# Re-ordering the fill work of a recurrent forward loop: unit scores, softmax and value products moved between the waits of a step, query turns taken off TensorE

## The chip, the cores and the metric

The program runs on one core of one Trainium2 chip. The metric is the device time of one launch in microseconds. Names of engines: PE is TensorE's matmul queue (PEld its weight loads), DVE is VectorE, ACT is ScalarE, POOL is GpSimd, SP is SyncE, which here only issues transfers. Lines such as L766 are lines of the kernel before.

## The reference

The kernel computes a forward pass and all its gradients. What matters here is one part of the forward pass, a recurrence over 64 segments of 32 tokens with a memory of 8 rows of width 640:

```python
for s in range(n_seg):                                   # 64 segments
    h = concat([mem, xs])                                # 8 memory rows + 32 tokens, 640 wide
    q, k, v = h @ Wq, h @ Wk, h @ Wv                     # 32 heads of 128
    p = softmax(where(mask, q @ k.T * Dh ** -0.5, -1e9)) # 40 x 40 for each head
    o = (p @ v) @ Wo
    mem = o[:8]                                          # the next segment needs these 8 rows
    outs.append(o[8:])
```

Each step needs the 8 memory rows that the step before produced. The token rows of a segment depend on the memory through keys and values alone, so most of their work can be done later.

## The kernel before, in words

Before the loop, queries, keys and values of the first 672 tokens are computed in full and stored in memory (QVX, KX). The loop (the function recurrence) has a chain for each of the 64 steps t. The chain takes hx, 32 columns: 8 memory rows and, riding along, 24 token rows of a later segment. It runs:

- projections (helper packed_half, L320, 20 matmuls of 512 columns for each half of a weight): first half of the values (sv0), two halves of the keys, two of the queries, second half of the values (sv1). Each half is copied out of its accumulator bank (bA, bB, bC) to a stage tile, and the stages are stored to QVS and KS by SP (the helper dump, L634);
- value_rows (L643), which puts the 8 memory rows of the values into the tile vt;
- packed_sel (L328), which turns the memory rows of keys and queries;
- the memory's own attention: scores (L676), copy sTm, turn (L686), softmax on DVE and ACT (the tile Pm, L697), turn (L311), values (L705), copies to oTm;
- the output projection, called the fold (L339, 64 matmuls), the sum of its halves fsz (L355), a turn (L370) and the copy into the next hx (L722).

Between these stand named gaps (W0, W1, V0, W2, G1 to G6). The function FILL puts other work into them, by the name of the gap. That work is the attention of the token rows, three segments to a tile and four heads to a unit (tile, quad): a tile of 120 rows has 8 units, and step t works on units of the tile before, by the table 0, 1, 2, then 3, 4, 5, then 6, 7. A unit goes through: ld of q and v rows (L265, L777, L245), turn_q (four PE turns of the queries, L788, and an ACT copy), scores (L800 to L805), soft_max and soft_exp (L813, L835), norm (L855, on POOL) with a store to PR, turn_p (L868), pv_mm (L888, L891), pv_turned and pv_rows with stores to OTX and OR. Keys of a later tile come by ld_k (tile kr, L265) and are turned by kprep (L766). The tiles oride and ride bring token columns for oTm and hx. Single matmuls on the identity (L945, the table WARM) are also put into gaps; nothing reads their result.

in_order fixes the order in which the code was written on each engine's queue, so every engine, SP with its transfers too, handles its instructions strictly one after the other, and one that waits holds up all behind it. The transfers issued by SP and ACT share eight completion counters in turn. The tile tag "oride" is one buffer for three things in a step: the stage sv0, then the loaded oride, then half of the fold's sum.

Of the kernel before, what the change touches and what calls it, by code (L numbers as in the profile page):

```python
# [9 lines left out]
BF16 = mybir.dt.bfloat16  # L10
# [6 lines left out]
P = 128  # L17
# [297 lines left out]
def packed_half(k, bank, x, W, b):  # L315

    for dc in range(k.DC):
# [258 lines left out]
def recurrence(k, W0, W4, Wv, Wk_, Wq, Wo, own, ps, banks):  # L576
    nc, tc = k.nc, k.tc
    D, DC, S, H, HD, T = k.D, k.DC, k.S, k.H, k.HD, k.T
    with tc.tile_pool(name="achain", bufs=1) as ch, \
# [7 lines left out]
        WARM = dict(G2=1, G3=2, G5=2)  # L587
# [33 lines left out]
        def chain(t, gap):  # L621
# [14 lines left out]
            def values(b, sv, bank):  # L636
                packed_half(k, bank, hx, Wv, b)
                k.copy(sv, bank[:], eng='s')
# [12 lines left out]
            dump(sv0, k.QVS[t // 4, :, :, t % 4, 1, 0:512])  # L651
            sq = stage()
            half(Wq, 0, sq, bA)
            dump(sk[:], k.KS[t // 4, :, :, t % 4])
            half(Wq, 1, sq, bB)
            qmT = ch.tile([P, H, 8], BF16, name="qmT", tag="fup")
            for sg, b_, dst, eng in ((sk, bC, kT[:, :, 40 * s:40 * s + 8], 's'), (sq, bA, qmT[:], 'v')):
                pk = bview(b_, P, 8, 4, 8)
                packed_sel(k, pk, sg, 0)
                packed_sel(k, pk, sg, 1)  # L660
                k.copy(dst.rearrange("p (g j) c -> p j g c", g=4), pk[:], eng=eng)
                if sg is sk:
                    gap("W1")
            dump(sq[:], k.QVS[t // 4, :, :, t % 4, 0])
            gap("V0")
            sv1 = stage()[:, 0:512]
            values(1, sv1, bC)
            value_rows(1, sv1)
            gap("W2")

            psT = bview(bA, P, 2, 8, 16)
            for h in range(H):
# [3 lines left out]
                nc.tensor.matmul(psT[0:m, h // 16, :, h % 16], k.kTT[:, o:o + m], qmT[:, h, :], start=True, stop=True)  # L676
            sTm = ch.tile([P, 2, P], BF16, name="sTm", tag="fup")
            nc.scalar.copy(sTm[:], psT.rearrange("p a q h -> p a (q h)"))
            if t + 1 < T:
                ride(t + 1)  # L680
            gap("G1")
            if t > 0:
                qm(t - 1)
# [69 lines left out]
        uu = {}  # L753

# [6 lines left out]
        def kprep(tl, qd, eng='s'):  # L761
            ns, nm, nx, n = k.geo(tl)
            kr = uu.pop(("kr", tl, qd))
            pt = ps.tile([P, 4, nx], BF16, name="kpt", tag="x", bufs=5)
            for j in range(4):
# [1556 lines left out]
```

## Time and profile before

| what | value |
|---|---|
| median of 3 runs | 4611.26 us (4608.62 to 4618.95) |
| the profiled execution's own time | 4624.73 us, its span 4623.0 us |
| granted TensorE clock, whole span | 0.983 |
| steps 0 to 63 of the loop | about 440 to 1540 us of the span |
| in 440 to 1540 us: busy PE, DVE, ACT, POOL | 997.8, 737.9, 593.0, 629.8 us of 1100 |
| transfers there | 0.63 of the transfer engines' time, 180 GB/s |

A row of the timeline gives start, duration, engine, line and operation, with the idle time before it and what ended it in brackets; rows of one form may be merged (x20). A PE duration includes the tail of the pipeline, so what a group costs in the queue is the distance from its start to the next start. Rows named SPq are transfers being issued; the duration is that of issuing, not of landing. Some matmul records are missing from a trace.

### The profile page before, as it was taken

Reading aid. Unit: us, or ns where it says so; the run is one execution under the profiler, and the core shown is the slowest. Engines: PE = TensorE matmul, PEld = TensorE weight load, DVE = VectorE, ACT = ScalarE, POOL = GpSimd, SP = SyncE. Lnnn points to the kernel's source line nnn. Section 1 sums busy time; section 2 is a strip of 40 time slices with the busy share of each in tenths; the row PEclk is TensorE's granted clock in tenths of the full one; section 3 lists DMA queues with packets and bytes.
Section 4 is the critical chain, followed back from the end, with each engine's and each line's share of the span. In section 5 each row is a group of like instructions: output and inputs, shape, how many; then the busy total and the mean of one; then the engine's idle time right before and its main releaser. Section 6 shows DMA issues by size and latency. Waiting matters only on the chain. (4 is left out here: it accounts for less than half of the span.)

```text
span 4623.0 us, 155683 instructions
## 1 busy us (share of the span) xinstructions
PE 4302.4 (93%) x62114; PEld 2828.5 (61%) x62336; DVE 2251.9 (49%) x7137; ACT 1615.4 (35%) x4509; POOL 2110.7 (46%) x3531
## 2 busy tenths in 40 slices
PE   8998998899999887999999998999999999999999
PEld 4544665565665545666666666577656766667665
DVE  8734666666666534555555553244223432311550
ACT  5532555555554523333333332133222322200000
POOL 6532555555565413555555554355334543211440
PEclk9999999999999998999999999999999999999999
DMA  7773666666665668788777776555435644589774
GB/s 263 241 253 110 183 180 180 185 182 184 182 180 171 169 156 240 220 230 226 222 224 219 221 206 163 114 159 148 128 105 141 163 130 110 154 227 211 166 173 100
DMA packets 986047, 834.55 MB, mean 181 GB/s; under 512 B 519914, under 2 KB 875694, under 8 KB 983360
## 3 DMA queue, kind: packets, MB, share of 16 engines
q1 hardware_dynamic: 754855, 531.10, 42.2%
q0 software_dynamic: 129952, 228.13, 17.0%
q10 hardware_dynamic: 100515, 65.34, 5.3%
q8 instruction: 493, 8.08, 0.7%
q14 instruction: 232, 1.90, 0.1%
HBM read 472.66 MB, written 310.33 MB: 169 GB/s over the span
## 5 line engine op out<-in xcount | busy, mean ns | idle before, releaser
L1697 PE MATMUL wg<-gr,hr 128*128 128x512 bf16 x2352 | 519.1, 379 | 2.5
L1678 PE MATMUL g<-land,ghacc 128*128 128x320 bf16 x3072 | 459.0, 300 | 0.8
L320 PEld LDWEIGHTS <-hx 128*32 128x32 bf16 x10240 | 266.5, 97 | 264.7 <-issue 27.5
L1697 PEld LDWEIGHTS <-hr 128*128 128x128 bf16 x2400 | 233.9, 98 | 278.9
L1678 PEld LDWEIGHTS <-ghacc 128*128 128x128 bf16 x3072 | 288.9, 98 | 103.8 <-ACT ghacc L92 2.2
L90 DVE CAST wgo<-wg 128x512 bf16<-128x512 f32 x72 | 49.8, 692 | 471.2 <-PE wg L1697 471.2
L908 POOL DMA_DIRECT2D OR<-xv x163 | 94.5, 580 | 335.6 <-ACT xv L92 290.5
L92 ACT COPY ghacc<-t6g 128x768 bf16<-128x768 bf16 (+1 forms) x176 | 137.2, 780 | 295.2 <-PE t6g L1660 284.8
L339 PEld LDWEIGHTS <-gkv 128*8 128x8 bf16 x8192 | 189.8, 87 | 81.9 <-issue 2.3
L1643 POOL DMA_DIRECT2D GSP<-grs x48 | 25.6, 543 | 456.4 <-ACT grs L1635 454.6
L628 DVE CAST stg<-bank 128x512 bf16<-128x512 f32 x256 | 168.4, 688 | 124.8 <-PE bank L320 108.5
L1354 POOL DMA_DIRECT2D VTD<-gvT x176 | 130.2, 749 | 198.4 <-ACT gvT L1353 182.5
L1684 DVE TENSOR_TENSOR ghacc<-ghacc,g 128x320 f32<-128x320 f32 x192 | 93.7, 488 | 209.8 <-PE g L1678 209.8
L92 ACT CAST wgo<-wg 128x512 bf16<-128x512 f32 x48 | 28.1, 586 | 479.8 <-PE wg L1697 406.9
L835 ACT ACTIVATE xP<-xsp,xnm 120x120 bf16<-120x120 f32 (+1 forms) x540 | 186.0, 367 | 17.8 <-DVE xnm L817 15.1
L855 POOL TENSOR_TENSOR xP<-xP,xrz 120x480 bf16<-120x480 bf16 x163 | 163.8, 1020 | 49.2 <-DVE xrz L854 39.4
L339 PE MATMUL bank<-Wo,oTm 128*32 128x320 bf16 x4032 | 159.2, 313 | 15.3 <-DVE oTm L90 14.1
L320 PE MATMUL bank<-WoT,hx 128*32 128x512 bf16 x2560 | 154.1, 388 | 11.3 <-DVE hx L1312 10.9
L1401 POOL DMA_DIRECT2D GXP<-gks x157 | 93.1, 593 | 155.4 <-ACT gks L1399 154.7
L320 PE MATMUL bank<-Wv,hx 128*32 128x512 bf16 x2560 | 161.6, 381 | 1.1 <-DVE hx L722 1.1
L351 ACT COPY fup<-bank 64x160 f32<-64x160 f32 (+1 forms) x190 | 57.4, 334 | 293.2 <-PE bank L339 288.5
L245 POOL DMA_DIRECT2D land<-QVS x256 | 144.9, 570 | 30.4 <-DMA land<-GOS 5.8
(399 smaller groups left out, 10924.5 us busy)
## 6 DMA issues: line engine op xcount, KB each, us to landing
kTT<-VTD SPq DMA_DIRECT2D x64, 320.0 KB
PR<-xP POOLq DMA_DIRECT2D x168, 120.0 KB, 3.0
VTD<-gvT POOLq DMA_DIRECT2D x168, 120.0 KB, 4.2
land<-DSR SPq DMA_DIRECT2D x168, 120.0 KB
land<-PR SPq DMA_DIRECT2D x168, 120.0 KB
OR<-xv POOLq DMA_DIRECT2D x163, 120.0 KB, 3.7
orr<-OR SPq DMA_DIRECT2D x14, 1280.0 KB
KS<-stg SPq DMA_DIRECT2D x64, 256.0 KB
```

Source lines behind the costliest of these rows:

```text
L92: return nc.scalar.copy(out, in_)
L245: eng.dma_start(d, src if src.shape[0] > 1 else src[0])
L320: k.nc.tensor.matmul(bank[32 * g:32 * g + 32, :], x[:, dc, :], W[:, dc, c0:c0 + 512], start=(dc == 0), stop=(dc == k.DC - 1), tile_positio ...
L339: k.nc.tensor.matmul(pm[a][p0:p0 + nq, 0:320], x[:, h, :], W[:, h, 320 * b:320 * b + 320], start=(first and i == 0), stop=(last and i == 1 ...
L628: nc.vector.tensor_copy(sg[:, b * 512:(b + 1) * 512], bank[:])
L835: nc.scalar.activation(Pb[0:n, j, 0:n], sp[0:n, j, :], ACT.Exp, bias=nmx[0:n, j:j + 1], scale=k.scale, accum_out=Z[0:n, j:j + 1])
L855: eng.tensor_tensor(Pb[0:n, :, 0:n], Pb[0:n, :, 0:n], bc_last(rz[0:n], n), ALU.mult)
L908: q.dma_start(k.OR[120 * tl:120 * tl + n, c0:c0 + 512], v[0:n])
L1354: nc.gpsimd.dma_start(k.VTD[tl][:, :, h0:h0 + 4, :], vTq[:])
L1678: nc.tensor.matmul(pg[:], ring[:, i, j, r0:r0 + P], Ws[qd][i][:, j, 320 * h:320 * h + 320], start=(i == 0 and j == 0), stop=(i == 2 and j ...
L1684: nc.vector.tensor_tensor(a, a, pg[:], ALU.add)
L1697: nc.tensor.matmul(pw[:], hr[:, tl, dc * P:(dc + 1) * P], grs[i][:, tl, :], start=(tl == 0), stop=(tl == NF - 1))
```

## The change

It rewrites FILL and what FILL calls; the arithmetic of the chain stays.

- Scores of the units of step t+1 are issued in G5 and G6 of step t (the wait for the fold's sum) rather than in G2 of their own step. Their softmax runs while the projections run (S0 to W3), with one exponential for each head in every unit; the variant with a subtraction for the third unit goes. Turns of the probabilities, value products and their stores come into G1 to G4.
- The queries of a unit are no longer loaded as rows and turned on PE: SP issues a crossbar transfer (DMA_TRANSPOSE) from QVS or QVX for 96 columns, and POOL copies the 24 memory columns from a tile qTm that the chain now keeps (q_mem).
- The memory rows of sv0 reach vt by four SP transfers rather than four DVE copies, and they stand ahead of the store of sv0.
- kprep of two units moves from G4 to G2, into bank bB, ahead of the turn of Pm (L311). The identity matmuls of G5 and, in steps with units, of G2 go.

```diff
-        WARM = dict(G2=1, G3=2, G5=2)
+        WARM = dict(G2=1, G3=2)
+        qTm = [ch.tile([P, H, 24], BF16, name=f"qTm{i}") for i in range(2)]
...
             def value_rows(b, sv):
                 for g in range(4):
                     p0, c0 = 64 * (g // 2), (g % 2) * 1024 + b * 512
-                    (nc.gpsimd if b == 1 and g % 2 else nc.vector).tensor_copy(vt[p0:p0 + 8, c0:c0 + 512], sv[32 * g:32 * g + 8])
+                    dst, src = vt[p0:p0 + 8, c0:c0 + 512], sv[32 * g:32 * g + 8]
+                    if b == 0:
+                        nc.sync.dma_start(dst, src)
+                    else:
+                        (nc.gpsimd if g % 2 else nc.vector).tensor_copy(dst, src)
+            gap("S0")
             sv0 = ch.tile([P, 512], BF16, name="sv0", tag="oride")[:]
-            values(0, sv0, bA)
+            packed_half(k, bA, hx, Wv, 0)
+            k.copy(sv0, bA[:], eng='s')
+            value_rows(0, sv0)
+            dump(sv0, k.QVS[t // 4, :, :, t % 4, 1, 0:512])
+            gap("S1")
             sk = stage()
             half(Wk_, 0, sk, bB)
-            value_rows(0, sv0)
             half(Wk_, 1, sk, bC)
             gap("W0")
...
+        def kprep(units, bank=None, eng='v'):
...
+            pt = ps.tile([P, m, nx], BF16, name="kpt", tag="x", bufs=5)[:] if bank is None else bview(bank, P, m, nx, bf=True)
...
+        def ld_q(tl, qd):
...
+            turned_load(k, qTs[i][:, :, 0:nx], src)
+        def q_mem(tl, qd, eng='g'):
...
+            k.copy(qTs[i][:, :, nx:n], qTm[tl % 2][:, 4 * qd:4 * qd + 4, 0:nm], eng=eng)
...
+            if g == "S0":
+                for i in range(3):
+                    at(soft_max, t, i)
+                at(lambda a, b: soft_exp(a, b, 0, 2), t, 0)
+                if t > 0:
+                    qm(t - 1)
+                at(ld_q, t + 1, 0)
...
+            elif g == "W0":
+                at(lambda a, b: norm(a, b, q=None), t, 0)
+                for i in range(2):
+                    at(ld_v, t, i)
+                at(norm_st, t, 0)
+            elif g == "W1":
+                at(lambda a, b: norm(a, b, q=None), t, 1)
+                at(norm_st, t, 1)
                 oride_ld(t)
+                at(ld_q, t + 1, 1)
...
+            elif g == "W4":
+                at(norm_st, t, 2)
                 ride_ld(t + 1)
+                at(ld_v, t, 2)
                 for u in kb[0:2]:
                     ld_k(*u)
+                at(ld_q, t + 1, 2)
             elif g == "G1":
+                at(lambda a, b: turn_p(a, b, 's'), t, 0)
+                at(lambda a, b: turn_p(a, b, 's'), t, 1)
                 oride(t)
...
+                at(pv_mm, t, 0)
+                at(pv_mm, t, 1)
+                at(turn_p, t, 2)
+                if kb:
+                    kprep(kb[0:2], bB)
+                at(pv_turned, t, 0)
+                at(pv_rows, t, 0)
...
+                for u in kb[2:]:
+                    kprep([u])
+                at(scores, t + 1, 0)
+                at(scores, t + 1, 1)
             elif g == "G6":
-                at(turn_p, t, 1)
-                at(pv, t, 0)
-                at(norm, t, 2)
+                at(scores, t + 1, 2)
```

Three places show how the order of instructions moves. The first is SP's queue in the middle of the loop, from the store of sv0 to the key rows kr of the same step. Before:

```order
L634 DMA QVS<-sv_19845 128x512
L634 DMA KS<-stg 128x1024
L634 DMA QVS<-stg 128x1024
L874 DMA oride<-OTX 128x768
L265 DMA kr<-KS 96x512 x2
```

In the change, from the four transfers of value rows to kr:

```order
L642 DMA vt<-sv_19576 8x512 x4
L635 DMA QVS<-sv_19576 128x512
L801 DMA xv<-QVM 24x512
L265 DMA xv<-QVS 96x512
L801 DMA xv<-QVM 24x512
L265 DMA xv<-QVS 96x512
L875 DMA oride<-OTX 128x768
L270 DMA_TRANSPOSE xqT_2978<-QVS 128x4x96
L635 DMA KS<-stg 128x1024
L635 DMA QVS<-stg 128x1024
```

and right behind these, in the same step:

```order
L801 DMA xv<-QVM 24x512
L265 DMA xv<-QVS 96x512
L265 DMA kr<-KS 96x512 x3
L635 DMA QVS<-stg 128x512
```

Between the store of sv0 and the first kr stood three transfers; now there are ten (eight in the steps with two units), one of them a crossbar turn. The load of oride writes the buffer that sv0's store and the four value transfers read, so it waits until all five have landed.

The second place is PE around the turn of Pm (L311). Before, key turns (kpt) come behind the memory's values (L705):

```order
L705 LDWEIGHTS vt
L705 MATMUL bank_4108<-PTm,vt 128x16
L766 LDWEIGHTS kr
L766 MATMUL kpt<-ident,kr 128x96
...
L339 LDWEIGHTS oTm
L339 MATMUL bank_4107<-Wo,oTm 32x320
```

In the change they come ahead of L311:

```order
L869 LDWEIGHTS xP_2983
L869 MATMUL xpp<-ident,xP_2983 128x120
...
L777 LDWEIGHTS kr
L777 MATMUL bank_4108<-ident,kr 128x96
...
L311 LDWEIGHTS Pm
L311 MATMUL bank_4109<-ident,Pm 128x128
```

The memory's chain (L311, then L705) now stands in PE's queue behind instructions that wait for the transfers of kr.

The third place is PE behind the fold. Before, turns of queries (qpt) and of probabilities (xpp) stood there:

```order
L788 LDWEIGHTS xq
L788 MATMUL qpt<-ident,xq 128x120
...
L868 LDWEIGHTS xP_2981
L868 MATMUL xpp<-ident,xP_2981 128x120
...
L370 LDWEIGHTS fsz
L370 MATMUL bank_4109<-sel,fsz 128x8
```

In the change a third key turn and the next step's scores:

```order
L777 LDWEIGHTS kr
L777 MATMUL kpt<-ident,kr 128x96
L815 LDWEIGHTS ident
L815 MATMUL xsp<-mask_88,ident 128x480
L818 LDWEIGHTS xqT_2980
L818 MATMUL xsp<-kTT,xqT_2980 128x24
```

The turns of queries are gone from PE's queue here, and more matmuls than before stand between the fold and the turn of its sum (L370).

More of the change, by code (lines that the diff above doesn't have):

```diff
@@ L312, in turn_pad, with packed_half @@
     k.nc.scalar.copy(dst[:].rearrange("p a q h -> p a (q h)"), ps3)
-def packed_half(k, bank, x, W, b):
-    for dc in range(k.DC):
+def packed_half(k, bank, x, W, b, d0=0, d1=None):
+    for dc in range(d0, k.DC if d1 is None else d1):
         for g in range(4):
@@ L652, in chain @@
             sq = stage()
             half(Wq, 0, sq, bA)
+            gap("W1")
+            pk = bview(bC, P, 8, 4, 8)
+            packed_sel(k, pk, sk, 0)
+            packed_sel(k, pk, sk, 1)
+            k.copy(kT[:, :, 40 * s:40 * s + 8].rearrange("p (g j) c -> p j g c", g=4), pk, eng='s')
             dump(sk[:], k.KS[t // 4, :, :, t % 4])
             half(Wq, 1, sq, bB)
[L656 to L663, printed above, removed]
+            pq = bview(bA, P, 8, 4, 8)
@@ L664, in chain @@
+            packed_sel(k, pq, sq, 0)
+            gap("W2")
+            sv1 = stage()[:, 0:512]
+            packed_half(k, bC, hx, Wv, 1, 0, 2)
+            packed_sel(k, pq, sq, 1)
+            qm_ = qTm[tl % 2][:, :, 8 * s:8 * s + 8]
+            k.copy(qm_.rearrange("p (g j) c -> p j g c", g=4), pq, eng='v')
+            packed_half(k, bC, hx, Wv, 1, 2, k.DC)
+            k.copy(sv1, bC[:], eng='s')
             dump(sq[:], k.QVS[t // 4, :, :, t % 4, 0])
-            gap("V0")
-            sv1 = stage()[:, 0:512]
@@ L667, in chain @@
-            values(1, sv1, bC)
+            gap("W3")
             value_rows(1, sv1)
-            gap("W2")
+            gap("W4")
             psT = bview(bA, P, 2, 8, 16)
@@ L675, in chain @@
                 o += 120 * H * (tl % 2)
-                nc.tensor.matmul(psT[0:m, h // 16, :, h % 16], k.kTT[:, o:o + m], qmT[:, h, :], start=True, stop=True)
+                nc.tensor.matmul(psT[0:m, h // 16, :, h % 16], k.kTT[:, o:o + m], qm_[:, h, :], start=True, stop=True)
             sTm = ch.tile([P, 2, P], BF16, name="sTm", tag="fup")
             nc.scalar.copy(sTm[:], psT.rearrange("p a q h -> p a (q h)"))
+            gap("G1")
             if t + 1 < T:
                 ride(t + 1)
-            gap("G1")
-            if t > 0:
-                qm(t - 1)
             ps2 = bview(bA, P, 2, 40)
@@ L759, in ld_k @@
             uu["kr", tl, qd] = kr
-        def kprep(tl, qd, eng='s'):
+        def kprep(units, bank=None, eng='v'):
+            tl, qd = units[0]
             ns, nm, nx, n = k.geo(tl)
-            kr = uu.pop(("kr", tl, qd))
-            pt = ps.tile([P, 4, nx], BF16, name="kpt", tag="x", bufs=5)
-            for j in range(4):
-                nc.tensor.transpose(pt[:, j, :], kr[0:nx, j * P:(j + 1) * P], k.ident[0:nx, 0:nx])
-            dst = kTs[tl % 2][:, qd * 4:qd * 4 + 4, 0:n].rearrange("p h (s c) -> p h s c", c=40)[:, :, :, 8:40]
-            k.copy(dst, pt[:].rearrange("p h (s c) -> p h s c", c=32), eng=eng)
@@ L778, in ld @@
             else:
[L779 to L790 removed]
+                k.load_m(r, tl, "v", c0, c0 + 512, eng)
@@ L792, in scores @@
+            k.load_x(r, 0, k.x_src(tl, "v", c0, c0 + 512), eng)
+            uu["v", tl, qd] = r
         def scores(tl, qd):
@@ L943, in gap @@
                         w_ld(2)
-                for i in range(WARM.get(g, 0) - (len(batch.get(t + 1, ())[1:2]) if g == "G5" else 0)):
-                    nc.tensor.matmul((bC if g == "G5" else bB)[:], k.ident[:], Wq[:, 0, 0:512], start=True, stop=True)
+                for i in range(WARM.get(g, 0)):
+                    if g == "G2" and batch.get(t):
+                        continue
+                    nc.tensor.matmul((bA if g == "G3" else bB)[:], k.ident[:], Wq[:, 0, 0:512], start=True, stop=True)
             return gap
```

167 lines of the change are left out of this document (65 added, 102 removed).

## The prediction

> **What bounds the kernel now.** I read the busy time by stage first, then PE's waits inside the loop, then one step on each engine's timeline.
>
> ```profile
> 440.00:1540.00 1100.00, 997.76 (x19911) 658.30 (x20022) 737.88 (x2029) 593.00 (x1950) 629.78 (x971) 0.99 0.63 180
> PE bank L311 <- DVE Pm L697: 33.1, 59, 1.4
> PE xpp L868 <- POOL xP L855: 15.2, 24, 2.8
> PE bank L339 <- DVE oTm L90: 13.9, 47, 0.8
> PE kpt L766 <- DMA kr<-KS: 1.0, 2, 0.8
> PE kpt L766 <- DMA kr<-KX: 0.7, 1, 0.7
> ```
>
> The first row is the loop's stretch (busy time of PE, PEld, DVE, ACT, POOL, granted clock, share and GB/s of transfers). The others are waits of PE there: sum, times, longest. The 64 steps are bound by PE's queue: it is busy for 998 of 1100 us at a clock of 0.99, and the largest waits are small stops of about half a microsecond inside the memory's chain. Key rows (kr) hardly ever hold PE up: three times in all. One step of PE:
>
> ```profile
> 1001.57 1.26 PE L320 MATMUL bank<-Wv,hx 128*32 128x512 bf16 x20
> 1009.34 0.96 PE L676 MATMUL bank<-qmT,kTT 128*128 128x8 bf16 x32
> 1010.76 0.22 PE L686 MATMUL bank<-ident,sTm 128*128 128x40 bf16 x2 [0.24 <-ACT sTm L678]
> 1010.83 0.36 PE L800 MATMUL xsp<-mask,ident 120*128 120x480 bf16 x1
> 1012.75 0.28 PE L311 MATMUL bank<-ident,Pm 128*128 128x128 bf16 x2 [0.33 <-DVE Pm L697]
> 1012.87 0.59 PE L945 MATMUL bank<-Wq,ident 128*128 128x512 bf16 x2
> 1014.06 0.51 PE L766 MATMUL kpt<-ident,kr 96*128 96x96 bf16 x8
> 1014.78 2.36 PE L339 MATMUL bank<-Wo,oTm 128*32 128x320 bf16 x64 [0.21 <-DVE oTm L90]
> 1017.07 0.59 PE L788 MATMUL qpt<-ident,xq 120*128 120x120 bf16 x8
> 1017.50 0.37 PE L868 MATMUL xpp<-ident,xP 120*128 120x120 bf16 x4
> 1019.05 1.26 PE L320 MATMUL bank<-Wv,hx 128*32 128x512 bf16 x20
> ```
>
> I call the first row's start S. The step takes 17.48 us (1019.05 - 1001.57). The memory's scores start at S+7.8, L686 at S+9.2, L311 at S+11.2, the fold at S+13.2; from L311 to the next S it is 6.3 us. The chain from L311 on (turn, values, fold, next hx) is strictly serial, so whatever moves L311 moves the step. And SP's queue in the same step:
>
> ```profile
> 1004.08 0.34 SPq L634 DMA_DIRECT2D QVS<-sv  x1
> 1006.49 0.34 SPq L634 DMA_DIRECT2D KS<-stg  x1
> 1007.92 0.32 SPq L634 DMA_DIRECT2D QVS<-stg  x1
> 1008.70 0.32 SPq L874 DMA_DIRECT2D oride<-OTX  x1
> 1009.07 0.92 SPq L265 DMA_DIRECT2D kr<-KS  x2
> 1018.88 0.31 SPq L777 DMA_DIRECT2D xv<-QVM  x1
> 1019.24 0.35 SPq L265 DMA_DIRECT2D xv<-QVS  x1
> ```
>
> kr is issued at S+7.5 and used at S+12.5: 5.0 us in which it can land. This margin is what the change spends.
>
> **What comes off PE.** Query turns: 32 in three steps, 10.7 a step. Eight cost 0.43 us (1017.07 to 1017.50), so 0.57 us a step. Identity matmuls: two fewer a step, each 0.2 us by the pair before L705 in the step above (0.43 us at most with what follows); these filled waits, so taking them out shortens nothing by itself. The scores move to the fold's wait as they are (1.4 us for three units, L800's start at S+9.3 to about S+10.7). Behind the fold stood 1.98 us (1017.07 to 1019.05) to the next step; with a key turn (0.22), two units of scores (0.95), the turn of the sum (0.16) and the third unit's scores (0.48) I get 1.8. The projections lose 0.1 to 0.4 us of value products that stood between them. Together the step would be shorter by 0.35 us (bounds 0.1 and 0.99, that is all of 0.57 and 0.42): over 61 steps 21 us (6 to 60). DVE and ACT don't gain or lose a place on the path by this: DVE's three softmax maxima (0.65 us and a small scaling each) fit into the 2.4 us before the first key half has to be copied, and ACT gives up the query copies (0.56) for two copies of turned probabilities of the same size.
>
> ```profile
> 1003.96 0.69 DVE L628 CAST stg<-bank 128x512 bf16<-128x512 f32 x1 [2.27 <-PE bank L320]
> 1012.61 0.65 DVE L813 TENSOR_REDUCE xmx<-xsp 120x4 f32<-120x480 f32 x1
> 1010.61 0.56 ACT L790 COPY xqT<-qpt 128x480 bf16<-128x480 bf16 x1
> ```
>
> **What the moved transfers cost.** kr's use moves from S+12.5 to right behind the value products. PE gets there at about S+10.8: L686 at S+9.1, then two units of value products, which wait for ACT's two copies of turned probabilities behind sTm, and a turn, together 1.7 us. So kr would have to be issued by S+7. Its place in SP's queue moves the other way. I add up that queue from rows:
>
> ```profile
> 1003.47 0.59 ACT L92 CAST sv<-bank 128x512 bf16<-128x512 f32 x1
> L270 SPq DMA_TRANSPOSE ride<-XN x16: 1222/1320/1842, 246.5 to 1408.1; - x16
> PR<-xP POOLq DMA_DIRECT2D x168, 120.0 KB, 3.0
> QVX<-b0st POOLq DMA_DIRECT2D x14, 128.0 KB, 2.1
> ```
>
> sv0's copy ended at S+2.5; now two exponentials stand ahead of it instead of a value copy, so S+2.3. Four value transfers at 0.38 each (0.33 like the xv rows above, and the gap): S+3.8. The store of sv0 is issued there. The load of oride waits for that store to land, because both use one buffer. The profile gives no landing times for SP's transfers; POOL's of this size take 3.0 us in this loop (PR) and 2.1 in a quiet stage (QVX), so oride goes out at S+6.8 (bounds S+5.9 and S+8.5, the latter by the 4.7 us below). What stood behind it and had to wait only for data now waits with it: a crossbar turn 1.3 us, stores of keys and queries 0.35 each, the third unit's values 0.8. kr is issued at S+10.0 (S+9.2 in the steps with two units). One step in four has a turn of ride ahead of it as well: 1.35 us more, 0.33 on average. How long kr then takes to land is bounded by the few cases where PE was seen to wait for it:
>
> ```profile
> 822.19 0.96 SPq L265 DMA_DIRECT2D kr<-KS  x2
> 826.42 0.51 PE L766 MATMUL kpt<-ident,kr 96*128 96x96 bf16 x8 [0.27 <-DMA kr<-KS]
> 1119.55 1.30 SPq L270 DMA_TRANSPOSE ride<-XN  x1
> 1120.90 1.06 SPq L265 DMA_DIRECT2D kr<-KS  x2
> 1125.79 0.34 PE L766 MATMUL kpt<-ident,kr 96*128 96x96 bf16 x4 [0.76 <-DMA kr<-KS]
> ```
>
> 4.2 us from the first issue in the one, 4.9 to the second half in the other, both with a turn of ride ahead. These are the late ones, since a landing that nobody waits for isn't seen; POOL's 3.0 is the other end. I take 3.7. So both kr are there at S+13.7 (S+12.9 with two units), the last four turns take 0.22, and L311 starts at S+13.9 (13.2) where Pm itself is ready at S+11.3. Against S+11.2 that is 2.7, 2.7 and 2.0 us in a group of three steps, 2.5 on average, 2.8 with ride. Less the 0.35 above: 2.5 us a step. It holds in the steps that load oride and have units, 7 to 62: 56 steps, 140 us. All of SP's slack behind kr is spent too, but the third key, vt and the next queries are wanted 4 us and more after their issue, so I cost them at nothing; if that cover goes, a late third key would add up to 1 us in two steps of three.
>
> **What a gap does to the clock.** PE then stands almost idle from S+10.8 to S+13.9 in every step. The trace shows what shorter stops do at times:
>
> ```profile
> 938.42 0.28 PE L311 MATMUL bank<-ident,Pm 128*128 128x128 bf16 x2 [1.21 <-DVE Pm L697]
> 940.44 4.03 PE L339 MATMUL bank<-Wo,oTm 128*32 128x320 bf16 x64 [0.21 <-DVE oTm L90]
> 934.00:946.00 12.00, 10.33 (x194) 7.48 (x185) 6.18 (x21) 7.24 (x28) 9.46 (x15) 0.86 0.73 206
> ```
>
> After a stop of 1.21 us in this stage the granted clock is 0.86 over 12 us and the fold takes 4.03 us rather than 2.36: 1.67 us lost. That is rare at such stops (the clock of the whole loop is 0.99), and the 2.8 us stop in the list of waits is among those without it; with 3 us in a thinly filled stage I take every second step: 0.5 x 1.67 x 56 = 47 us. The Trainium skill says on its page TensorE: Matmul & The Clock Gate, in the section Why this matters for your kernels, that PE should have no idle gaps above about 3 us between bursts, or the clock falls back to half. By that rule it would be every step, 94 us; the case has a chance of its own below.
>
> **The sum** for the profiled execution: 4624.7 + 140 + 47 = 4812 us, of which 4623.0 was span. It stood 13.5 us above the median of the runs shown, so for the median 4611.3 + 187, rounded to **4795 us**.
>
> **The rivals.**
>
> 1. The same mechanism, but small. If SP issues faster (oride at S+5.9, the 2.1 us row) and kr lands in 3.0, L311 is at S+12.3 and 11.6: about 1.1 us late with ride, 0.75 net, 42 us, and few clock drops, 10 us: 4660. For it: landing times of SP were never seen directly. Against: both terms at their low ends at once.
> 2. The other side: the key rows are in time. If kr were issued before oride's wait bites, at S+7 as before, L311 keeps its place and only the work taken off PE counts: 21 us, at most 60, so 4590 (4550 to 4605). It decides at an issue by S+7. For it: in the step above sv0's store had 4.6 us until oride went out at 1008.70, and oride went out nearly when the queue reached it. Against: ten transfers between, one of 1.3 us, and the row order is fixed.
> 3. The clock falls in every step, and the projections behind it start at half speed too: 94 us and as much again in a third of the steps: 140 + 94 + 31, so 4875. Against: the stop of 2.8 us that did not do it.
> 4. The gain and the late keys cancel, within 0.2%: 4611. It needs L311 late by only 0.35 us on average.
>
> A bound by ACT or DVE is no case: both are below 70% busy, and the moved pieces are as large as those that go.
>
> **Chances.** My forecast 0.57, with its own range 4715 to 4860; rival 1 0.17; rival 2 0.11; rival 3 0.10; rival 4 0.05. About 0.2% (9 us) is what a measurement can tell here from no change. Faster 0.11, same 0.05, slower 0.84. The range reaches into rival 1 and to rival 3: 4625 to 4885 leaves out rivals 2 and 4 and a little above.
>
> **What would show it.** In the changed kernel, the largest wait of PE in the loop should be that of the two key turns for kr, some 2 to 3 us in nearly every step, and L311 should no longer wait for Pm. SP's timeline should show oride going out 6 to 8 us after S, a turn of 1.3 us behind it and kr at S+9 to S+11. The fold should take 4 us in about half of the steps, and the loop some 20 us a step. If L311 still waits for Pm and kr isn't among PE's waits, the forecast is wrong at its root; if the kr wait is 1 us, the price of the landing was.

## The result, and the profile after it

The changed kernel takes **4928.19 us** (median of 4 runs, 4914.89 to 4939.15) against 4613.03 us before (4608.62 to 4618.95, run beside it): a ratio of **1.068, 95% interval 1.065 to 1.071**, 315 us slower. The forecast was 4795 with a range up to 4885, so the sign was right and the size was not. The profiled execution took 4914.89 us.

The head of its page: span, busy time by engine, and the granted clock in 40 slices.

```profile
span 4913.2 us, 154110 instructions
PE 4378.0 (89%) x61504; PEld 2869.0 (58%) x61504; DVE 2152.7 (44%) x6757; ACT 1553.5 (32%) x4640; POOL 2133.6 (43%) x3679
PEclk9998888888887888899999999999999999999999
```

The slices 4 to 17, in which the forward loop lies, have lost clock. The loop as one stage (busy time of PE, PEld, DVE, ACT, POOL, then the clock, share and GB/s of transfers):

```profile
440.00:1840.00 1400.00, 1083.13 (x19311) 707.13 (x19304) 643.94 (x1672) 538.72 (x2095) 651.11 (x1110) 0.84 0.56 141
```

PE's waits in the same stretch (sum, times, longest):

```profile
PE bank L693 <- ACT sTm L687: 178.4, 38, 6.3
PE bank L693 <- DMA xv<-QVS: 55.2, 11, 6.2
PE bank L693 <- DMA kr<-KS: 15.6, 3, 5.6
PE bank L693 <- DMA kr<-KX: 14.5, 3, 5.1
PE bank L311 <- DVE Pm L704: 1.8, 6, 0.4
```

The loop now needs some 1400 us where it needed 1100, and PE is idle for more than 300 of them. L693 is the product that turns the memory's scores (L686 before). It waits 264 us by the first four rows, 281 with two smaller ones: 178 are put down to sTm, which it reads, the rest to transfers that ended during the same wait. The two key turns (L777), the forecast's place, are not among PE's largest waits. L311 waits no longer for Pm, as forecast, but not on account of kr: it follows L693 by 2.8 us where it was 2.1, with value products and key turns between them, and that is longer than Pm takes.

Who is late for sTm shows in all engines' waits in that stretch, and then in two steps on ACT's timeline:

```profile
DVE vt L644 <- ACT stg L92: 362.9, 60, 7.6
PEld L693 <- ACT sTm L687: 295.5, 60, 6.5
ACT stg L92 <- DMA KS<-stg: 293.3, 42, 8.7
```

```profile
1101.76 0.59 ACT L92 CAST stg<-bank 128x512 bf16<-128x512 f32 x1 [6.32 <-DMA KS<-stg]
1102.24 0.38 ACT L687 CAST sTm<-bank 128x256 bf16<-128x256 f32 x1
...
1125.31 0.59 ACT L92 CAST stg<-bank 128x512 bf16<-128x512 f32 x1 [7.87 <-DMA KS<-stg]
```

The cast ahead of sTm's is the copy of sv1, the second value half. Its tile has the tag "stg", which has two buffers, and the step uses three such tiles in turn: keys (sk), queries (sq), values (sv1). So sv1 takes sk's buffer, and ACT waits until the store of the keys has landed. sTm stands behind it in ACT's order. The end of that step on PE's timeline, and the next one on SP's queue:

```profile
1102.67 0.25 PE L693 MATMUL bank<-ident,sTm 128*128 128x40 bf16 x2 [4.65 <-ACT sTm L687]
...
1105.01 0.93 PE L777 MATMUL bank<-ident,kr 96*128 96x96 bf16 x8
...
1107.84 2.38 PE L339 MATMUL bank<-Wo,oTm 128*32 128x320 bf16 x64
...
1112.23 1.05 PE L320 MATMUL bank<-Wv,hx 128*32 128x512 bf16 x16 [0.29 <-DVE hx L729]
```

```profile
1114.32 2.67 SPq L642 DMA_DIRECT2D vt<-sv  x4
1117.04 0.44 SPq L635 DMA_DIRECT2D QVS<-sv  x1
...
1119.37 0.34 SPq L875 DMA_DIRECT2D oride<-OTX  x1
1119.76 1.22 SPq L270 DMA_TRANSPOSE xqT<-QVS  x1
1121.03 0.57 SPq L635 DMA_DIRECT2D KS<-stg  x1
1121.64 1.24 SPq L635 DMA_DIRECT2D QVS<-stg  x1
1122.92 0.90 SPq L265 DMA_DIRECT2D kr<-KS  x2
```

S of this step is 1112.23. The four value transfers take 2.67 us of SP's queue, oride goes out at S+7.1, a crossbar turn of 1.22 us follows, and only then, at S+8.8, the key store, whose landing lets ACT go on at 1125.31. The keys had been copied long before: in the kernel before, their store went out at 1006.49, S+4.9.

Below, the mean place of some instructions in a step, worked out from the timelines of PE and SP over the steps that start between 500 and 1500 us (54 before, 43 after; us behind S, and e1 to e14 are the experiments that follow):

```
                            before  after   e1     e2     e5     e8     e10    e11    e12    e14
step                         18.54  23.47  23.18  21.23  19.96  22.75  19.21  19.13  18.48  18.33
memory's scores               8.11   7.77   7.75   8.25   8.25   8.25   8.24   8.26   8.26   7.77
their turn (L686, L693)       9.65  13.97   9.31  11.19  10.91   9.74   9.78   9.75   9.76   9.36
L311                         11.73  16.78  15.73  14.21  13.59  12.31  12.63  11.79  12.02  11.77
fold (L339)                  13.92  18.95  18.01  16.36  15.59  16.97  14.64  14.10  14.09  14.06
fold to next S                4.62   4.52   5.17   4.87   4.37   5.78   4.57   5.03   4.39   4.27
key store issued by SP         5.4    9.9      -    6.9    6.7    4.9    5.1    5.0    5.1    4.6
oride issued                   7.1    8.0    8.2    5.1    7.3   11.5    7.9    7.8    7.8    7.6
```

Of 4.93 us a step, 4.32 come up at the turn of the memory's scores and 0.73 from there to L311; the rest of the step is unchanged. 4.93 x 61 steps is 301 of the 315 us.

### The profile page after: what moved, and what is told of

It reads as the page before. It is cut to its first block, busy times and chain, and to the rows that moved or that the text cites. A ratio compares the mean times of both kernels' runs of the same rounds, so it can differ in the third digit from the quotient of the medians.

```text
span 4913.2 us, 154110 instructions
## 1 busy us (share of the span) xinstructions
PE 4378.0 (89%) x61504; PEld 2869.0 (58%) x61504; DVE 2152.7 (44%) x6757; ACT 1553.5 (32%) x4640; POOL 2133.6 (43%) x3679
## 4 chain that ended last, share of the span: by engine, by line
PE 67%; DMA 10%; issue 9%; DVE 6%; ACT 3%; POOL 3%; SPq 1%; ACTq 0%; POOLq 0%; DVEq 0%
PE bank L339 11%; PE wg L1708 11%; PE g L1689 8%; PE bank L320 8%; PE oa L1855 4%; PE wa L2243 2%; PE b0pb L384 2%; PE r6p L1639 2%; DMA KS<-stg 2%; PE t6g L1671 2%; PE w2a L2099 1%; DMA ggtok<-ggT 1%; PE bank L1274 1%; DMA sl<-SLT 1%; PE bank L328 1%
## 5 line engine op out<-in xcount | busy, mean ns | idle before, releaser
L320 PEld LDWEIGHTS <-hx 128*32 128x32 bf16 x10240 | 253.9, 97 | 243.1 <-issue 24.7
L838 ACT ACTIVATE xP<-xsp,xnm 120x120 bf16<-120x120 f32 (+1 forms) x704 | 243.4, 369 | 140.8 <-DVE xnm L830 109.0
L693 PE MATMUL bank<-ident,sTm 128*128 128x40 bf16 x128 | 15.7, 205 | 291.0 <-ACT sTm L687 183.8
L339 PEld LDWEIGHTS <-gkv 128*8 128x8 bf16 x8192 | 189.4, 87 | 81.7 <-issue 3.2
L644 POOL COPY vt<-stg 8x512 bf16<-8x512 bf16 x128 | 82.3, 643 | 320.9 <-ACT stg L92 318.3
L644 DVE COPY vt<-stg 8x512 bf16<-8x512 bf16 x128 | 56.6, 442 | 372.8 <-ACT stg L92 372.0
L339 PE MATMUL bank<-Wo,oTm 128*32 128x320 bf16 x4032 | 182.7, 342 | 6.2 <-POOL xqT L94 5.3
L693 PEld LDWEIGHTS <-sTm 128*128 128x128 bf16 x128 | 8.3, 109 | 301.3 <-ACT sTm L687 301.3
L320 PE MATMUL bank<-Wv,hx 128*32 128x512 bf16 x2560 | 174.1, 382 | 6.6 <-DVE hx L729 6.6
```

What stands on the lines that cost most here:

```text
L320: k.nc.tensor.matmul(bank[32 * g:32 * g + 32, :], x[:, dc, :], W[:, dc, c0:c0 + 512], start=(dc == 0), stop=(dc == k.DC - 1), tile_positio ...
L339: k.nc.tensor.matmul(pm[a][p0:p0 + nq, 0:320], x[:, h, :], W[:, h, 320 * b:320 * b + 320], start=(first and i == 0), stop=(last and i == 1 ...
L644: (nc.gpsimd if g % 2 else nc.vector).tensor_copy(dst, src)
L838: nc.scalar.activation(Pb[0:n, j, 0:n], sp[0:n, j, :], ACT.Exp, bias=nmx[0:n, j:j + 1], scale=k.scale, accum_out=Z[0:n, j:j + 1])
```

## Experiments

Theory A: SP's queue is late in every step, and what the chain needs next from it sets the step. Its rivals are told with each run; the main ones were that the clock sets it, that the four value transfers cost by themselves, and that the new order of the work on the engines is what is dear.

**The key store on ACT's queue (e1).** It takes the key store out of SP's queue and nothing else.

```diff
-            dump(sk[:], k.KS[t // 4, :, :, t % 4])
+            dump(sk[:], k.KS[t // 4, :, :, t % 4], nc.scalar)
```

> The change (4928 us), but the store of the two key halves (KS from the stage tile) is issued by ACT right behind the copy of the turned keys, and no longer by SP behind oride and the crossbar turn. Theory A: the change is slow because SP's queue gets to its transfers late, and the first who suffers is not PE's key turn but the stage tile: it has two buffers, the second half of the values (sv1) takes the one of the keys, and its copy on ACT waits for the KS store, which goes out only at S+8.8, to land. With the store out at about S+5.5 the wait of L693 for sTm (291 us in the loop) falls under 60 us, and then the wait that was forecast shows: PE waits 1.5 to 2.5 us a step for the key rows kr. Time 4770 to 4830. Rival B (all transfers land late, from the load that crossbar turns put on the transfer engines): still above 4890, sTm still late. Rival C (ACT's own queue is too full to bring sTm in time): one more issue on ACT makes it 4928 to 4960.

Measured: 4908.55 us, ratio 1.063 (1.061 to 1.066). PE's waits in 440 to 1840:

```profile
PE bank L777 <- DMA kr<-KS: 164.1, 55, 5.4
PE bank L777 <- DMA kr<-KX: 52.8, 22, 5.5
PE bank L693 <- ACT sTm L687: 7.9, 10, 1.6
```

The wait for sTm is gone (7.9 us where L693 stood 281), and the forecast's wait stands in its place: the two key turns wait for kr, 217 us. The time fell by only 20 us, far below the expected 100 to 160: two late transfers hang on one queue, and the earlier wait had hidden the later one. Removing the earlier alone gains next to nothing. The later wait stands right ahead of the memory's chain, and the folds (64 matmuls of L339) show it: 39 of the 43 in the steps from 500 to 1500 us took over 3 us, 3.47 on the mean; before it was 3 of 54, 2.46 on the mean.

**The value rows back on VectorE (e2).** The four transfers of sv0's rows go, as four copies, where they were before; all else is as changed.

```diff
-                    if b == 0:
-                        nc.sync.dma_start(dst, src)
-                    else:
-                        (nc.gpsimd if g % 2 else nc.vector).tensor_copy(dst, src)
+                    (nc.gpsimd if b == 1 and g % 2 else nc.vector).tensor_copy(dst, src)
...
             half(Wk_, 0, sk, bB)
+            value_rows(0, sv0)
             half(Wk_, 1, sk, bC)
```

> The change, with the memory rows of sv0 copied to vt by four DVE copies as before, not by four SP transfers. In the change the four take 2.7 us of SP's time (0.66 each, 0.38 were forecast). Theory A: everything behind them in SP's queue goes out 2.7 us earlier, so the KS store lands at about S+9 and kr at about S+12; L693's wait falls from 4.8 us a step to about 1.5, few waits for kr; 3 to 4 us less in each of 57 steps: 4700 to 4760. Rival B (crossbar turns slow all landings): under 40 us gained, 4890 or more. A rival in between (each us of SP's queue is only part of the wait, the rest sits on ACT): 4780 to 4860.

Measured: 4784.94 us, ratio 1.038 (1.035 to 1.040), 143 us off, in the range of the rival in between; the key store goes out at S+6.9 instead of S+9.9. Both waits shrink together and neither goes (440 to 1700):

```profile
PE bank L690 <- ACT sTm L684: 61.2, 37, 3.2
PE bank L774 <- DMA kr<-KS: 28.1, 26, 2.8
PE bank L328 <- DVE stg L629: 26.8, 60, 0.5
```

**The same part alone, in the kernel before (e6).** Its four copies of sv0's rows become four transfers on SP's queue.

```diff
-                    (nc.gpsimd if b == 1 and g % 2 else nc.vector).tensor_copy(vt[p0:p0 + 8, c0:c0 + 512], sv[32 * g:32 * g + 8])
+                    dst, src = vt[p0:p0 + 8, c0:c0 + 512], sv[32 * g:32 * g + 8]
+                    if b == 0:
+                        nc.sync.dma_start(dst, src)
+                    else:
+                        (nc.gpsimd if g % 2 else nc.vector).tensor_copy(dst, src)
```

> The kernel before with one part of the change alone: the four copies of the first value rows are made by SP's queue (four transfers) instead of VectorE and GpSimd. Theory A (four transfers of 0.66 us are worth what they delay behind them; in the kernel before, kr has 5.0 us to land and needs about 3.7, so 2.6 us of delay eats the margin and a little more): 4620 to 4680, with a small wait for kr, at most 60 us in the loop. Rival B (the four transfers cost what they cost in the changed kernel, by their own load on the rings): 4740 to 4780, that is 4618 + 143.

Measured: 4644.34 us against 4614.02, ratio 1.0065 (1.0043 to 1.0087): 30 us, where the changed kernel had paid 143 for the same four transfers. They take 0.65 us each here (208 transfers, 135.2 us of issuing from 500 to 1500 us), 2.9 us a step with the gaps between them. So most of the 143 us is not a price of their own: it depends on what is queued behind them and has no margin left. The wait that grew most is the one that the change brought, in small (PE's waits in 440 to 1700; it was 11.5 us before):

```profile
PE bank L690 <- ACT sTm L682: 33.0, 41, 3.2
```

**All query turns at the step's start (e3).**

```diff
                     qm(t - 1)
-                at(ld_q, t + 1, 0)
+                for i in range(3):
+                    at(ld_q, t + 1, i)
```

(and the two later calls gone)

> The change, with all three crossbar turns of the next step's queries issued at the start of the step (gap S0), where SP stands idle waiting for sv0; the number of turns is the same, and none stands between sv0's transfers and the KS store. Theory A: only the 1.25 us of issuing between oride and KS counts; KS and kr go out 1.3 us earlier, 57 x 1.3 = 74 us less: 4840 to 4870. Rival B (the turns as such load the transfer engines and delay landings): no change, 4915 to 4945. Rival D (the three turns now delay sv0's transfers instead): slower than 4945.

Measured: 4900.62 us, ratio 1.062 (1.060 to 1.064). L693 still waits:

```profile
PE bank L693 <- ACT sTm L687: 191.0, 44, 6.7
```

Taking 1.3 us from in front of the key store gave 28 us and not 60 to 90: the turns are still SP's work, and now delay the value transfers (S+2.7, it was S+2.1), so that the key store goes out at S+9.2 where it was 9.9.

**Filling the gap for the clock (e4).** Twelve identity matmuls ahead of L693, in the steps that have units.

```diff
-        WARM = dict(G2=1, G3=2)
+        WARM = dict(G1=12, G2=1, G3=2)
...
-                    if g == "G2" and batch.get(t):
+                    if g == "G2" and batch.get(t) or g == "G1" and not batch.get(t):
                         continue
```

> The change, with twelve matmuls on the identity, whose result nothing reads, put on PE into the wait ahead of L693 (12 x 0.2 = 2.5 us of a wait of 4.8 us at full clock), so they lengthen no step by themselves. It measures the clock alone. The granted clock of the loop is 0.85 in the change, one window of 3.4 us at half speed in each step. Theory A: the clock rises above 0.93 and the fold and what follows L693 run at full speed: 0.7 to 1.2 us less a step, 40 to 70 us, 4860 to 4890. Rival (what follows L693 is bound by copies on DVE and ACT, so the clock costs nothing): 4915 to 4945 with the clock up.

Measured: 4943.23 us, ratio 1.071 (1.068 to 1.073). The loop's row:

```profile
440.00:1840.00 1400.00, 1223.90 (x20029) 743.61 (x20029) 642.65 (x1676) 541.38 (x2109) 651.55 (x1107) 0.91 0.56 141
```

The clock rose from 0.84 to 0.91 and the step stayed as long (23.40 against 23.47). The changed kernel's clock record has 7.3 us a step at half clock, not the 3.4 of the expectation, and e4 has 4.1. But the folds did not get faster: 15 of 43 took over 3 us, where it was 12 of 43. So this fill gained nothing; what a full clock behind L693 would be worth here, it does not show.

**All early demands off SP's queue (e5).** e2, and the query turns and the first two key loads at the step's start, and oride's load behind the second query half.

```diff
                     qm(t - 1)
-                at(ld_q, t + 1, 0)
+                for i in range(3):
+                    at(ld_q, t + 1, i)
+                for u in kb[0:2]:
+                    ld_k(*u)
...
             elif g == "W2":
+                oride_ld(t)
```

> The changed kernel with all its early demands on SP's queue taken away: the first value rows by VectorE again, the three query turns and the two key loads at the very start of the step (ahead of the stores), the load of oride behind the second query half. Theory A (the loss is SP's queue being late, and what waits on it): the wait of L693 for sTm and the wait for kr both go below 60 us in the loop, the granted clock there is back at 0.93 or more, and the time is 4590 to 4690. Rival B (the new order of the work on PE, ACT and DVE costs by itself, the queue only hides it): SP's waits go, but the time stays at 4720 to 4790, about that of the run with the rows alone on VectorE (4785).

Measured: 4727.47 us, ratio 1.025 (1.023 to 1.026). Theory A's figure was missed, the rival's was met; but PE's waits (440 to 1700) say why, and so does SP's queue in the step with S at 1099.83:

```profile
PE bank L690 <- ACT sTm L684: 70.7, 36, 4.6
PE bank L311 <- DVE Pm L701: 29.1, 40, 1.3
```

```profile
1098.78 4.90 SPq L270 DMA_TRANSPOSE xqT<-QVS  x3
1103.72 1.04 SPq L265 DMA_DIRECT2D kr<-KS  x2
1104.86 0.37 SPq L635 DMA_DIRECT2D QVS<-sv  x1
...
1107.96 0.38 SPq L635 DMA_DIRECT2D KS<-stg  x1
```

kr is no longer among the larger waits, but the key store still goes out at S+8.1 in this step (S+6.7 on the mean): three turns, two key loads, a store and four value loads now stand ahead of it.

**e2 with the key store on ACT (e7).**

```diff
-            dump(sk[:], k.KS[t // 4, :, :, t % 4])
+            dump(sk[:], k.KS[t // 4, :, :, t % 4], nc.scalar)
```

> The changed kernel with the first value rows by VectorE and the store of the keys issued by ScalarE: takes away both the four transfers and the wait of the second value copy for the key store. Theory A (two waits that hang on one queue; each shows the other when it is removed alone): the 62 us of L693 behind sTm go, kr's wait of 28 us stays or grows to at most 60, time 4710 to 4780. Rival B (what is left of e2's loss is not these waits): 4780 to 4800, no gain.

Measured: 4763.24 us, ratio 1.031 (1.029 to 1.033). As in e1 the removal of one wait brings the other up: L690's wait for sTm falls to 23 us, kr's is 75 in two rows (56.3 and 18.4), more than the 60 expected; the time is in the expected range.

**The key store first, in two ways (e8, e10).** Both are e5 with the key store right behind the second key half, ahead of the value loads. In e10 the three turns stay at the step's start; in e8 they stand in the gap W1, which in the code is behind the first query half (not the second, as the expectations say), ahead of oride's load.

```diff
             half(Wk_, 1, sk, bC)
+            dump(sk[:], k.KS[t // 4, :, :, t % 4])
             gap("W0")
...
-            dump(sk[:], k.KS[t // 4, :, :, t % 4])
             half(Wq, 1, sq, bB)
```

> The run with the early demands taken off SP's queue (4727), and in it the key store issued right behind the second key half, ahead of the value loads, and the three query turns behind the second query half instead of at the step's start. In that run the key store still went out at S+8.1 and L690 stood for sTm 70.7 us in the loop (L690 1.3 us later in the step than before: 10.9 against 9.65); L311 followed L690 by 2.7 us against 2.1. Theory A (that wait is the rest of the loss): L690 back at S+9.4, its wait below 20 us, time 4640 to 4665 (4727 less 61 x 1.2). Rival B (value products and the key turn between L690 and L311 are the rest): L690 earlier but L311 not, time 4700 or more. Rival C (a new wait on SP's queue, by the turns before the key rows or oride): a wait of the same size elsewhere, 4700 to 4740.

> The run with the early demands taken off SP's queue (4727) with one edit: the key store right behind the second key half, ahead of the value loads. The three query turns stay at the step's start. Against the run where they stood behind the second query half (4887, a wait for values of the third unit and for oride instead) only their place differs. Theory A (SP's queue is a sum; what is issued behind a turn comes late, whatever it is): the key store goes out at S+5.4, L690 stands at S+9.5 to S+9.8 as there, and no new wait comes since only the value loads move by 0.4 us: 4640 to 4665. Rival B (key store first is itself what made the later transfers late): waits for values as there, 4800 or more.

Measured: e8 4886.82 us, ratio 1.060 (1.057 to 1.062); e10 4670.94 us, ratio 1.014 (1.011 to 1.017). In both the store goes out at S+5 and L690 stands at S+9.8 as in the kernel before (9.65), so the wait for the stage buffer is all but gone. The 4.5% between them come from the place of three crossbar turns alone. PE's waits in e8 (440 to 1700), and its queue in the step with S at 1043.93:

```profile
PE bank L339 <- POOL oTm L877: 42.8, 17, 3.6
PE xot L886 <- DMA xv<-QVS: 38.3, 15, 4.4
PE xot L886 <- DMA xv<-QVX: 37.8, 14, 4.6
```

```profile
1052.45 4.82 SPq L270 DMA_TRANSPOSE xqT<-QVS  x3
1057.36 0.53 SPq L872 DMA_DIRECT2D oride<-OTX  x1
1057.98 0.39 SPq L635 DMA_DIRECT2D QVS<-stg  x1
1058.53 0.32 SPq L798 DMA_DIRECT2D xv<-QVM  x1
```

Behind 4.82 us of turns, oride leaves at S+13.4 and the third unit's values at S+14.6, where the fold should start at S+14. Rival C of e8, a new wait by the order of the queue, held in kind, but its 4700 to 4740 was far too low. Part of the rest is the clock: in e8 42 of 45 folds took over 3 us, in e10 11 of 48, and from the fold to the next step it took 5.78 us against 4.57, that is 1.2 of the 3.5 us between the two steps. The order on PE, ACT and DVE is the same in both kernels. e10 came out a little above its 4640 to 4665.

**e8 with the key turn behind L311 (e9).**

```diff
             elif g == "G2":
...
-                if kb:
-                    kprep(kb[0:2], bB)
...
             elif g == "G3":
+                if kb:
+                    kprep(kb[0:2], bA)
```

> The same, with the turn of the two key tiles (8 transposes, 0.85 us, and its copy) behind L311 instead of ahead of it, where two identity matmuls stood. Theory A: L311 comes 0.4 to 0.5 us earlier behind L690, 25 us below the run with the keys first: 4615 to 4640. Rival B (PE is not what L311 waits for there; Pm's chain is): no difference of 10 us or more to that run.

Measured: 4879.34 us, ratio 1.057 (1.054 to 1.060), 7 us below e8, so rival B held: in e9 L311 waits 47 us for Pm (28 in e8), and oride and the values set the step as in e8.

**Value rows behind the softmax, key turn behind L311 (e11), on e10.** The key turn moves as in e9.

```diff
-            value_rows(1, sv1)
+            value_rows(1, sv1, (1, 3))
...
+            value_rows(1, sv1, (0, 2))
             gap("G2")
```

> That kernel with two more edits between L690 and L311: VectorE's two copies of the second value rows go behind the memory's softmax (in the steps looked at they took 0.9 to 1.8 us ahead of its first reduction), and the turn of the two key tiles goes behind L311. Theory A (with SP in time, the rest of the loss is the longer way from L690 to L311, 2.6 us against 2.1): L311 at S+11.6 to S+11.9, 25 to 60 us below the run before it, so 4590 to 4630, at or a little below the kernel before. Rival B (the copies only move to in front of the values at L709, which wait for them): no gain, 4640 to 4665.

Measured: 4659.17 us, ratio 1.013 (1.010 to 1.017). L311 came 0.84 us earlier (S+11.8 against S+12.6), and 0.08 us a step of it was left: the fold came only 0.54 earlier, and from there to the next step it took 0.46 longer. In 20 of the 45 folds whose 64 matmuls stand in one row, they took 4.0 us, in the others 2.42 (3 of 51 before). Ahead of the slow ones PE was idle 1.9 us between L690 and the fold, in pieces, ahead of the others 1.0.

**e11 with those short waits filled (e12).** Two identity matmuls ahead of L311, where e11 had none in steps with units, and one ahead of the values (L709, in e11 and e12 L710) in steps with key tiles, where it had none.

```diff
-        WARM = dict(G2=1, G3=2)
+        WARM = dict(G2=2, G3=2)
...
-                for i in range(WARM.get(g, 0)):
-                    if g == "G2" and batch.get(t) or g == "G3" and kbatch.get(t):
-                        continue
+                for i in range(WARM.get(g, 0) - (1 if g == "G3" and kbatch.get(t) else 0)):
```

> The run with the value rows behind the softmax (4659), and in it one or two identity matmuls more in PE's two short waits, ahead of L311 and ahead of the values at L709. In that run 20 of 45 folds whose 64 matmuls stand in one row took 4.0 us and the others 2.42; ahead of the slow ones PE stood idle 1.9 us between L690 and the fold, ahead of the fast ones 1.0. Theory A (what is left of the loss is the granted clock behind these gaps: 20/45 x 1.6 us x 61 steps = 43 us of the 46 to 59): slow folds below 10 in 45, and 4610 to 4640. Rival B (as in the changed kernel itself, filling raises the clock and gains nothing, since something else sets the step): 4650 to 4670.

Measured: 4627.91 us, ratio 1.0047 (1.0030 to 1.0065). One slow fold in 51. The loop's rows, first of e11, then of e12:

```profile
440.00:1540.00 1100.00, 975.78 (x18547) 620.98 (x18540) 647.59 (x1841) 529.16 (x2030) 623.39 (x1075) 0.95 0.67 172
```

```profile
440.00:1540.00 1100.00, 993.41 (x19215) 625.34 (x19275) 667.24 (x1904) 544.38 (x2092) 642.49 (x1104) 0.99 0.70 176
```

A fill gave nothing in the changed kernel (e4: twelve matmuls, ahead of L693, and slow folds as before). Here, with the transfers in time, a much smaller one close to the fold is worth 0.9% by the ratios, 31 us by the medians: the slow folds are gone and the clock is 0.99 again.

**The first value rows out of the second key half's way (e13, e14), on e12.** In e13 VectorE copies them behind the first query half, in e14 GpSimd does.

```diff
             half(Wk_, 0, sk, bB)
-            value_rows(0, sv0)
             half(Wk_, 1, sk, bC)
...
             half(Wq, 0, sq, bA)
+            value_rows(0, sv0)
```

> The run with the fill (4628), with VectorE's four copies of the first value rows (1.2 us) behind the copy of the first query half instead of ahead of the second key half. In that run L328 waits for that key half 28 us in 61 steps, in the changed kernel it waits far less since the rows are SP's there. Theory A (the rows on VectorE cost their 0.45 us a step in front of L328, and this is the 15 us that are left): the wait goes to 5 us or less, 4600 to 4615, at or below the kernel before. Rival B (the copies then delay the second query half and with it the memory's queries): L682 stays at S+8.25, 4620 to 4640.

```diff
-                    (nc.gpsimd if b == 1 and g % 2 else nc.vector).tensor_copy(dst, src)
+                    (nc.gpsimd if b == 0 or g % 2 else nc.vector).tensor_copy(dst, src)
```

> The run with the fill (4628), with the first value rows copied by GpSimd, which stands 4 us for VectorE's reciprocal at that time (four copies of about 0.62, 2.5 us). Theory A: VectorE is free for the second key half, L328's wait goes to 5 us or less, L682 at S+7.8, 4600 to 4615. Rival B (GpSimd's copies slow VectorE's at the same time, or delay the normalisation): no gain, 4620 to 4640.

Measured: e13 4621.61 us, ratio 1.0023 (1.0010 to 1.0036), its wait at L328 not gone (31.8 us) and L682 still at S+8.2, so rival B; e14 4616.06 us, ratio **1.0008 (0.9995 to 1.0021)**. In e14 L328 is not among PE's larger waits, and the memory's scores stand at S+7.8. No difference to the kernel before can be told: the loss is accounted for. The step is 0.2 us shorter than before (18.33 against 18.54), too little to show.

What the runs give back, in per cent of the time before: 3.1 by the value rows (e2), 1.3 by the place of the query turns, key loads and oride (e5), 1.0 by the key store (e10), 0.1 by L311 (e11), 0.9 by the clock (e12), 0.4 by the copies at L328 (e14). That is 6.7 of 6.8. The shares hold in this order of removal; e6 shows that the first, alone, is worth 0.65.

## Why the prediction was right and wrong

**Right: the mechanism.** SP's queue is late and the chain waits for what comes out of it. oride was to go out 6 to 8 us behind S and does at 8.0; the turn behind it was put at 1.3 us and takes 1.31 on the mean; L311 no longer waits for Pm.

**In part: the gain.** The memory's scores start 0.34 us earlier, but not because of the work taken off PE. In e2, e5, e10 and e12, with the first value rows back on VectorE, they start at S+8.25, later than before (8.11); in e14, with these rows on GpSimd, at 7.77 as in the changed kernel. It is VectorE that was freed for the second key half, where the forecast said that DVE doesn't gain a place on the path. Behind the fold there is a gain: in e14 the way from it to the next step is 0.35 us shorter (4.27 against 4.62), where the forecast had about 0.2 for this stretch. But from the scores to the fold e14 takes 0.48 us longer. Its step is 0.2 us shorter in the profiled execution, where the sum had 0.35, and its time is no shorter.

**Wrong: the first victim.** The step that failed is "What stood behind it and had to wait only for data now waits with it: a crossbar turn 1.3 us, stores of keys and queries 0.35 each". It costs the stores as issue time and follows only what is loaded. A store also frees a buffer, and the key store's buffer is the one that sv1 needs 3 us later. The edit moved that store from S+5.4 to S+9.9, and sv1's copy, then sTm behind it in ACT's order, then L693 waited 281 us in the loop. kr's wait, the forecast's, was behind it and could not be seen until e1 took the first away. Three tiles of one tag with two buffers stood in the code that was shown; the rotation was not followed.

**Wrong: the size, also of the wait that was forecast.** The first victim decides little of the time, since e1, without it, is only 20 us faster. In e1, where the forecast's wait does set the step, L311 stands 4.0 us late (15.73 against 11.73) and not 2.5. kr was issued at S+11.9, not at S+10.0, and the pieces are these: the term "Four value transfers at 0.38 each", gap included, measured 0.70 each, so sv0's store went out at S+4.8 instead of S+3.8, although the first of the four left 0.3 us sooner than forecast (1.0 us); oride 3.4 us behind it instead of 3.0 (0.4); kr 3.7 us behind oride instead of 3.2 (0.5). The price of kr's landing, 3.7 us, was met: 11.9 + 3.7 is S+15.6, where L311 is at 15.7. The gap to oride is for the most part not the landing of sv0's store as the forecast had it: value loads of 0.34 us each fill it in the quoted step, and in e1 SP stood idle 0.6 us ahead of oride on the mean. The forecast set 140 us for the delay; 4.0 us in 61 steps are 244. One bound of the forecast, oride at S+8.5 "by the 4.7 us below", has no such row (they give 4.2 and 4.9); the sum does not use it. The price of the four transfers was taken from loads of values out of DRAM; SP's queue had no transfer from tile to tile in this loop before.

**The clock.** The sum had a fold of 4 us in every second step, 47 us. In the changed kernel 12 of 43 folds took over 3 us and the mean fold took 2.80 us against 2.46: 0.34 us, 21 us in the loop. The long wait stands ahead of L693 there, 5 us before the fold. In e1 it stands where the forecast had it: 39 of 43 folds took over 3 us, and from the fold to the next step it takes 0.65 us longer than in the changed kernel (5.17 against 4.52), 40 us in the loop and near the forecast's 47. So rival 3 (4875) came nearest in its number by luck: it asks 94 and 31 us of the clock, and the folds of the changed kernel give 21. The Trainium skill's page TensorE: Matmul & The Clock Gate, section Why this matters for your kernels, wants no idle gaps above about 3 us; e11 differs from it: its slow folds stand behind 1.9 us of idle time in all, on the mean, and filling it made 20 slow folds in 45 into 1 in 51.

**The rivals.** Rival 1 needed both terms at their low ends; the queue was slower than forecast, not faster. Rival 2, key rows in time, is what e5 and e10 made true by moving the loads, and neither was a gain: in e5 the key store was still late, in e10 the clock and the copies at L328 were still to pay. Rival 4 did not come near.

## What to carry to other kernels

Before an edit puts transfers on a queue, write down for each transfer behind them both what reads it and what waits for its buffer; a store is as urgent as the next writer of its buffer, and in a rotation of buffers that writer is found by counting tiles. Where several transfers hang on one late queue, removing one wait only uncovers the next (e1 and e7 gained 20 to 30 us each by taking away what looked like a wait of 281 and most of one of 61): move the queue's order as a whole, and judge by the place of the chain's instructions in the step, not by the sum of one wait. Judge a fill of PE's gaps by the matmuls behind the last wait, not by the mean clock: e4 raised the clock from 0.84 to 0.91, left the folds slow and gained nothing; e12 made the folds fast and gained 0.9%.

## What the runs showed of the hardware

A small transfer can take longer to issue than a large one. 8 rows of 1 KB from one tile to another held SP's queue for 0.66 us (172 of them, 112.8 us, in the changed kernel; 0.65 in e6); in the step shown the store of sv0, 128 rows of 1 KB, took 0.44 and oride's load 0.34. Whether the few rows or the way from tile to tile make it dear was not tried. The crossbar turn of a 96-row query tile held it for 1.31 us (114 of them, 148.8 us), and for 1.32 in e10, where three are issued in a row; a row x3 of the timeline is longer, since it includes the gaps between them.

What is issued right behind a turn takes longer to issue too (medians). The key store took 0.57 us in the changed kernel, where a turn stands ahead of it, 0.42 in e3, where oride's load does, and 0.34 before and in e10. oride's load took 0.53 in e8, behind the three turns, and 0.36 in e10. Why is open.

Issue time on SP, summed over single transfers, rose from 10.0 to 13.3 us a step by the change and was 10.8 in e10; the four transfers of value rows (2.6 us) make up the difference between the last two. The Trainium skill's page DMA: Bandwidth & Descriptors, section Issuing engines are not separate DMA queues, says that issuing on several engines only saves the time of issuing, which is usually small relative to the DMA itself. In this loop it was not small: 13.3 us of a 23.5 us step.
